# Down projection of a gated block by 26 block products, accumulated in PSUM over all features

## The chip, the cores and the metric

The kernel runs on one core of a Trainium2 chip. The time is the device time of one execution in microseconds, here the median of several executions. Five engines matter. TensorE (PE in the profile) multiplies matrices into PSUM banks. VectorE (DVE), ScalarE (ACT) and GpSimd (POOL) do the elementwise work, and SyncE (SP) issues most of the DMA transfers between HBM and SBUF. Each engine works through its own instructions in order, and semaphores order them against each other.

## The reference

Two branches are computed from one token matrix `x` (2048 tokens, 576 columns), and a gate per token mixes them. The change touches only the second branch, the gated MLP:

```python
def _B_ref(x, w_gate, w_up, w_down):
    g = jnp.einsum("bsd,df->bsf", x, w_gate)
    u = jnp.einsum("bsd,df->bsf", x, w_up)
    h = _gelu(g) * u                              # 2048 x 4608
    return jnp.einsum("bsf,fd->bsd", h, w_down)   # 4608 -> 576

g = _sigmoid((x * gate_w).sum(-1, keepdims=True))
return g * a + (1 - g) * b      # a: linear attention, b: _B_ref
```

All data are float32.

## The kernel before

**Precision.** Every float32 operand of TensorE is split into a high part, rounded to TensorE's format by a ScalarE copy, and a low part, the difference of the value and its high part, by a subtraction on VectorE or GpSimd. A product is then three chains of matmuls: high by high, high by low, low by high.

**Stages.** First come the attention branch's projections, then a mixing stage whose steps are written out by hand in `PLAN`, which also leaves the gated attention result in DRAM (`ga_d`, one tile for each of 16 token tiles of 128). Then comes the gate/up stage: the loop over `CHAINS` (L998), one chain for each token half `p` (two halves, each of two blocks of 512 tokens), feature group `n` (18 groups of 256 features, two blocks of 128) and matrix `m` (`GATE` or `UP`). A chain is one 2x2 block product by seven block products (Strassen-Winograd), seven steps `s1` to `s7` in `gu_steps`. After an `UP` chain the four blocks of h of that half and group are known. The steps form the seven operand sums that the next product needs (L877 to L889) and store them block by block in DRAM (`keep_block`, `h_d`).

**The down stage** (L1053 to L1106) has 84 units: six slices `s` of three feature groups, two token halves `p`, seven products `k`. A unit multiplies a stored sum of h blocks (three groups of 128 features by 512 tokens) by a sum of blocks of `w_down` (three groups by 288 columns): four token tiles of nine matmuls, 36 matmuls of 128x128 by 128x288. For each unit

- `h_load` brings the h sum from DRAM (768 KB) into a raw buffer, through SyncE's queue;
- `h_make` splits it: a ScalarE copy (L966) and a VectorE subtraction (L967), both 1536 wide, into one of five buffers `hb`;
- `d_make` splits the weight sum: a ScalarE copy 864 wide (L946) and two GpSimd subtractions 432 wide (L948), into one of eight buffers `wd`. This is done once per slice and product, and serves both token halves;
- `d_sum` forms the weight sums T1 to T4 on GpSimd (L953), four per slice.

The h operands are made three units ahead of their use. At the end of a unit each of its four token tiles is read out of PSUM. For the first product the sum is copied to a second bank by ScalarE (L1069). For the six others VectorE multiplies the bank by `1 - g`, adds it to an accumulator in SBUF and writes it back (L1073); the accumulators `acc` start as the gated attention result. After the last slice the accumulators go to the output by DMA.

The order of the work is the order in which this program emits it: on each engine `unit(u, 0)`, then `h_make(u + 3)` and the load for u + 6, then `unit(u, 1)`, then the weight work. In the last gate/up chains the tables `D_AT` and `H_AT` place the first units' operand work between the steps.

Of the kernel before, what the change touches and what calls it, by code (L numbers as in the profile page):

```python
# [57 lines left out]
SEQUENCE = (1, 6, 2, 7, 5, 4, 3)  # L58
# [6 lines left out]
def tile_gated_mix(ctx, tc, xt, xs, xn, wk, wv, wq, wo, wgu, wdn, cst, out):  # L65
# [14 lines left out]
    h_d = [[dram.tile([128, 7, 3, BS], F32, name=f"h_d{p}_{i}") for i in range(NF2 // 3)] for p in range(NP)]  # L80
# [488 lines left out]
    nc.vector.tensor_scalar(gate[:, 1], gate[:, 0], -1.0, 1.0, op0=OP.mult, op1=OP.add)  # L569
    query(2, 2)  # L570
# [182 lines left out]
    def g_():  # L753
        nc.scalar.activation(probe, probe, AF.Gelu_apprx_tanh)
# [3 lines left out]
    def open_(k):  # L758
        if k == 0:
            turn.close()  # L760
            weights.close()
            pools["r3"] = mixing.pool("r3p")
            pools["q"] = mixing.pool("qp", bufs=2)
            pools["xc"] = chunks.pool("xcp", bufs=2)
        elif k == 1:
            aheads.close()
            proj.close()
            wgp = mlp.pool("wgp", side="right")
            W.extend(wgp.tile([128, 7, 5, 128], F32R, name=n) for n in ("wg", "wu"))
        else:  # L770
            chunks.close()
            pool = mlp.pool("mid", side="right")
            mid.update((k, pool.tile([128, BS], F32, name=k)) for k in ("p1", "u2", "u3", "e0"))
            es.append(mid["e0"])
            first_steps.extend(gu_steps(*CHAINS[0], first=True))
# [11 lines left out]
    POS = {PRODUCTS[k][0]: i for i, k in enumerate(SEQUENCE)}  # L787
# [3 lines left out]
    last_up = xf[:, 5184:9664].rearrange("p (a b c) -> p a b c", a=7, b=5)  # L791
# [27 lines left out]
    def gu_steps(p, n, m, first=False):  # L819
# [10 lines left out]
        def keep_block(a, src):  # L830
            nc.sync.dma_start(h_d[p][n // 3][:, POS[a], n % 3], src)
# [19 lines left out]
        def s2():  # L851
# [4 lines left out]
            else:  # L856
                up(0, a)
                keep_block(A11, es[0])
# [6 lines left out]
        def s5():  # L865
# [3 lines left out]
            if m == UP:  # L869
                keep_block(A22, es[3])  # L870

        def s4():
# [3 lines left out]
            if m == UP:  # L876
                nc.vector.tensor_tensor(sx[:, 0], es[2], es[3], OP.add)  # L877
                nc.vector.tensor_tensor(sx[:, 1], sx[:, 0], es[0], OP.subtract)
                nc.vector.tensor_tensor(es[2], es[0], es[2], OP.subtract)
                keep_block(S1, sx[:, 0])  # L880
                keep_block(S2, sx[:, 1])
                keep_block(S3, es[2])

        def s3():
# [3 lines left out]
            if m == UP:  # L888
                nc.vector.tensor_tensor(sx[:, 2], es[1], sx[:, 1], OP.subtract)  # L889
                keep_block(A12, es[1])  # L890
                keep_block(S4, sx[:, 2])
# [29 lines left out]
    DG = 6  # L921
    ORDER = (1, 2, 3, 4, 5, 0)
    UNITS = [(s, p, k) for s in range(DG) for p in range(NP) for k in range(7)]
# [8 lines left out]
    wd = [wd_view(xf[:, i * 1728:(i + 1) * 1728]) for i in range(4)]  # L932
    hb = [h_view(v) for v in (xf[:, 9984:13056], xf[:, 13056:16128], wf[1][:, :3072], wf[0][:, :3072], xf[:, 6912:9984])]
    hraw = [f32(xf[:, 16128:17664]).rearrange("p (g c) -> p g c", g=3), e123]
    draw = stage.rearrange("p (i c) -> p i c", i=5)
    D12, D11, D21, D22, DX = range(5)
    DAT = {B11: D11, B21: D21, B22: D22, T1: D11, T2: DX, T3: D12, T4: D21}

    def d_fetch(s):
        nc.sync.dma_start(draw[:, :4], wdn[ORDER[s]].rearrange("p i g c -> p i (g c)"))  # L940

    HALVES = slice(0, 432), slice(432, 864)

    def d_make(s, k):
        w, src = wd[(7 * s + k) % 8], draw[:, DAT[PRODUCTS[SEQUENCE[k]][1]]]
        nc.scalar.activation(w[:, 0], src, AF.Copy)  # L946
        for c in HALVES:
            nc.gpsimd.tensor_tensor(w[:, 1, c], src[:, c], f32(w[:, 0, c]), OP.subtract)  # L948

    def d_sum(t):  # L950
        o, x, y = {T1: (D11, D12, D11), T2: (DX, D22, D11), T3: (D12, D22, D12), T4: (D21, D21, DX)}[t]
        for c in HALVES:
            nc.gpsimd.tensor_tensor(draw[:, o, c], draw[:, x, c], draw[:, y, c], OP.subtract)  # L953

    def raw_of_h(j):
        return hraw[j % 2 if j < 4 else (j - 2) % 3]

    def h_load(j):
        if j < len(UNITS):
            s, p, k = UNITS[j]  # L960
            nc.sync.dma_start(raw_of_h(j), h_d[p][ORDER[s]][:, k])

    def h_make(j):
        if j < len(UNITS):
            h, raw = hb[j % 5], raw_of_h(j)
            nc.scalar.activation(h[:, 0], raw, AF.Copy)  # L966
            nc.vector.tensor_tensor(h[:, 1], raw, f32(h[:, 0]), OP.subtract)  # L967
# [17 lines left out]
    for k in range(2):  # L985
# [3 lines left out]
    D_AT = {(LAST - 2, 0): lambda: d_make(0, 0), (LAST - 2, 4): lambda: d_sum(T1), (LAST - 1, 0): lambda: d_sum(T2),  # L989
            (LAST - 1, 2): lambda: d_make(0, 1), (LAST - 1, 4): lambda: d_make(0, 2), (LAST - 1, 6): lambda: d_sum(T3),  # L990
            (LAST, 4): lambda: d_sum(T4)}
    W_AT, REST = {(0, 4): ((0, 2),), (0, 5): ((4, 6),)}, ((2, 3), (3, 4), (6, 7))
    H_AT = [(LAST - 1, 1), (LAST - 1, 3)]
# [4 lines left out]
    for c, chain in enumerate(CHAINS):  # L998
        for i, step in enumerate(first_steps if c == 0 else gu_steps(*chain)):
# [22 lines left out]
            if (c, i) == (LAST - 4, 0):  # L1022
                d_fetch(0)
            if c == LAST - 2 and i in (0, 4):
                h_load(i // 4)
            if (c, i) in D_AT:
                D_AT[c, i]()
            if (c, i) in H_AT:
                j = H_AT.index((c, i))
                h_make(j)  # L1030
                h_load(2 + j)
# [4 lines left out]
    acc = [dp.tile([128, 4, 4, 288], F32, name=f"acc{p}") for p in range(NP)]  # L1036
    wd += [wd_view(dp.tile([128, 1728], F32R, name=f"wd{i}")) for i in range(4)]
    hraw.append(dp.tile([128, 3, BS], F32, name="hraw"))

    def acc_load(p, t):  # L1040
        i, j = divmod(t, 4)
        nc.sync.dma_start(acc[p][:, 2 * i:2 * i + 2, j], ga_d[p * 8 + t].rearrange("p (n c) -> p n c", n=2))

    h_load(4)
    for t in range(4):
        acc_load(0, t)

    C11, C12, C21, C22 = range(4)
    RESULT = {6: C12, 2: C11, 7: C22, 5: C22, 4: C21, 3: C12}
    FINAL = {2: C11, 5: C22, 4: C21, 3: C12}  # L1050
    sums_of = {}

    def unit(u, q):  # L1053
        s, p, i = UNITS[u]
        k = SEQUENCE[i]
        name = {1: "a", 6: "b", 2: "a", 7: "b", 5: "d", 4: "b", 3: "d"}[k]
        h, w = hb[u % 5], wd[(7 * s + i) % 8]
        c = RESULT.get(k)
        ops = [(hl, wl, g) for hl, wl in ((0, 0), (0, 1), (1, 0)) for g in range(3)]
        for t in (2 * q, 2 * q + 1):  # L1060
            if k in (1, 5):
                sums_of[name, t] = bank()
            y = sums_of[name, t][:, :288]
            for n, (hl, wl, g) in enumerate(ops):
                nc.tensor.matmul(y, h[:, hl, g, t * 128:(t + 1) * 128], w[:, wl, g * 288:(g + 1) * 288],  # L1065
                                 start=k in (1, 5) and n == 0, stop=n == len(ops) - 1, skip_group_check=True)
            if k == 1:
                sums_of["b", t] = bank()
                nc.scalar.activation(sums_of["b", t][:, :288], y, AF.Copy)  # L1069
            else:  # L1070
                st = p * 8 + c // 2 * 4 + t
                o = acc[p][:, c, t]
                nc.vector.scalar_tensor_tensor(o, y, gate[:, 1, st:st + 1], o, op0=OP.mult, op1=OP.add)  # L1073
                if s == DG - 1 and FINAL.get(k) == c:
# [106 lines left out]
```

## Time and profile before

| | |
|---|---|
| runs | 1473.12, 1472.52, 1471.91 us; median 1472.52 |
| profiled execution, span from first to last instruction | 1470.6 us |
| TensorE busy | 1465.0 us |
| VectorE, GpSimd, ScalarE busy | 1038.5, 720.9, 547.2 us |
| HBM read, written | 156.84 MB, 88.28 MB |

The profiled execution is one execution, with a span of 1470.6 us; the time of a run is taken around the whole program and is 1.9 us longer at the median. In the profile's rows PE is a matmul, PEld the loading of its weights, L1065 a line of the kernel, `out<-in` the tiles that an instruction writes and reads; "x84" is a count. A row of windows gives the start and end of the stretch, its length, the busy time of PE, PEld, VectorE, ScalarE and GpSimd with their counts, the granted TensorE clock, the mean busy share of the 16 DMA engines and GB/s. A row by source line gives the shortest, median and longest duration in ns. A row of the timeline gives start, duration, engine, line and operation, and in brackets the idle time before it and what ended that.

### The profile page before, as it was taken

The numbers are of one execution on the slowest core, as the hardware profiler recorded it, in microseconds if no ns is written. First come the engines' busy times: TensorE is split into PE (matmuls) and PEld (weight loads), VectorE is DVE, ScalarE is ACT, GpSimd is POOL, SyncE is SP. The second block draws the span as 40 slices with busy tenths as digits, with TensorE's granted clock in tenths as the row PEclk, the third lists the DMA queues.
The fourth block names the chain that finished last, engine by engine and source line by source line (L and its number), as shares of the span: only waits on it lengthen the run. The fifth ranks groups of instructions, "written<-read, shape, count | busy, mean of one in ns | idle before, by whom it ended". The sixth has DMA issues, their size and how long they took to land.

```text
span 1470.6 us, 21605 instructions
## 1 busy us (share of the span) xinstructions
PE 1465.0 (100%) x8312; PEld 1311.9 (89%) x8312; DVE 1038.5 (71%) x1351; ACT 547.2 (37%) x719; POOL 720.9 (49%) x522
## 2 busy tenths in 40 slices
PE   9999999999999999999999999999999999999999
PEld 9999899888888888888888888888899999999999
DVE  7887898565677655677665677665778777777775
ACT  7555656333322223222223222232254444443431
POOL 1664543456455464465464464462446464463710
PEclk9999999999999999999999999999999999999999
DMA  7564476653333222333222333224796655565563
GB/s 255 160 207 140 161 250 218 238 220 129 108 143 143 108 103 108 112 143 144 94 107 107 123 143 126 103 109 182 263 344 213 218 173 204 169 221 199 175 215 127
DMA packets 100599, 246.56 MB, mean 168 GB/s; under 512 B 9416, under 2 KB 36616, under 8 KB 98320
## 3 DMA queue, kind: packets, MB, share of 16 engines
q1 hardware_dynamic: 97760, 237.91, 46.6%
q10 hardware_dynamic: 2736, 7.28, 1.3%
q8 instruction: 65, 1.06, 0.3%
q14 instruction: 38, 0.31, 0.1%
HBM read 156.84 MB, written 88.28 MB: 167 GB/s over the span
## 4 chain that ended last, share of the span: by engine, by line
PE 98%; DMA 1%; DVE 1%; ACT 0%; SPq 0%; issue 0%; DVEq 0%
PE bank L801 54%; PE bank L1065 27%; PE bank L479 4%; PE pair L728 4%; PE pair L282 2%; PE kpair L282 2%; PE pair L237 2%; PE kpair L237 2%; PE den L667 1%; DMA xn<-xn 0%; DMA raw<-wk 0%; PE pair L634 0%; PE pair L530 0%; DVE e L246 0%; ACT pkh L252 0%
## 5 line engine op out<-in xcount | busy, mean ns | idle before, releaser
L801 PE MATMUL bank<-xo,wg 128*128 128x512 f32 x1764 | 403.7, 389 | 0.0
L801 PEld LDWEIGHTS bank<-xo,wg 128*128 128x128 f32 x1764 | 330.8, 188 | 68.9 <-DVE f L835 0.3
L801 PE MATMUL bank<-xo,wu 128*128 128x512 f32 x1715 | 391.8, 389 | 0.0
L801 PEld LDWEIGHTS bank<-xo,wu 128*128 128x128 f32 x1715 | 321.9, 188 | 66.8
L1073 DVE SCALAR_TENSOR_TENSOR acc<-bank,gate,acc 128x288 f32<-128x288 f32 x288 | 139.9, 512 | 67.1 <-PE bank L1065 64.8
L321 POOL TENSOR_TENSOR stage<-stage 128x384 f32<-128x384 f32 x132 | 153.7, 1185 | 49.0 <-ACT ga L735 23.2
L844 ACT ACTIVATE p<-bank 128x512 f32<-128x512 f32 x72 | 43.0, 597 | 325.2 <-PE bank L801 204.9
L816 POOL TENSOR_TENSOR wg<-stage,wg 128x768 fp32r<-128x768 f32 (+3 forms) x37 | 73.8, 1996 | 164.8 <-ACT wg L815 163.3
L816 POOL TENSOR_TENSOR wu<-stage,wu 128x768 fp32r<-128x768 f32 (+1 forms) x34 | 76.5, 2251 | 141.7 <-ACT wu L815 140.4
L1065 PE MATMUL bank<-wd,xo 128*128 128x288 f32 x1008 | 136.2, 295 | 0.0
L1065 PEld LDWEIGHTS bank<-wd,xo 128*128 128x128 f32 x1008 | 134.4, 188 | 0.0
L948 POOL TENSOR_TENSOR xo<-stage,xo 128x432 fp32r<-128x432 f32 x44 | 65.0, 1498 | 112.7 <-ACT xo L946 84.0
L849 DVE TENSOR_TENSOR u<-bank,p 128x512 f32<-128x512 f32 x72 | 49.4, 686 | 89.0 <-PE bank L801 81.2
L1065 PE MATMUL bank<-xo 128*128 128x288 f32 x792 | 107.0, 295 | 0.2 <-DVE u L838 0.2
L1065 PEld LDWEIGHTS bank<-xo 128*128 128x128 f32 x792 | 105.6, 188 | 0.5 <-DVE u L838 0.4
L948 POOL TENSOR_TENSOR wd<-stage,wd 128x432 fp32r<-128x432 f32 x40 | 59.4, 1510 | 90.1 <-ACT wd L946 72.3
L835 DVE TENSOR_TENSOR f<-bank,u 128x512 f32<-128x512 f32 x54 | 37.2, 691 | 69.2 <-PE bank L801 68.8
L825 ACT ACTIVATE f<-f 128x512 f32<-128x512 f32 x54 | 34.1, 632 | 128.6 <-DVE f L835 128.6
L863 DVE TENSOR_TENSOR u<-bank,u 128x512 f32<-128x512 f32 x72 | 49.8, 692 | 38.1 <-PE bank L801 34.1
L953 POOL TENSOR_TENSOR stage<-stage 128x432 f32<-128x432 f32 x48 | 76.3, 1616 | 0.0
L825 ACT ACTIVATE e<-e 128x512 f32<-128x512 f32 x54 | 34.0, 631 | 91.9 <-DVE e L835 91.9
L835 DVE TENSOR_TENSOR e<-bank,u 128x512 f32<-128x512 f32 x54 | 37.1, 691 | 40.4 <-PE bank L801 39.0
(198 smaller groups left out, 2373.2 us busy)
## 6 DMA issues: line engine op xcount, KB each, us to landing
h_d<-sx SPq DMA_DIRECT2D x108, 256.0 KB, 7.7
stage<-wgu SPq DMA_DIRECT2D x34, 768.0 KB
xo<-h_d SPq DMA_DIRECT2D x29, 768.0 KB, 6.9
e<-h_d SPq DMA_DIRECT2D x28, 768.0 KB, 4.2
hraw<-h_d SPq DMA_DIRECT2D x27, 768.0 KB, 4.1
h_d<-e SPq DMA_DIRECT2D x72, 256.0 KB, 2.0
h_d<-f SPq DMA_DIRECT2D x72, 256.0 KB, 2.0
stage<-wdn SPq DMA_DIRECT2D x6, 1728.0 KB, 9.6
```

Of the source, the lines that this page charges most:

```text
L237: nc.tensor.matmul(out_t[:, :n], xa, kvw[i][:, r, lo:lo + n], start=(k == 0), stop=(k == 13))
L282: nc.tensor.matmul(y[:, n, :KH], a, p[:, n * KH:(n + 1) * KH], start=(k == 0), stop=(k == len(ops) - 1))
L321: nc.gpsimd.tensor_tensor(o, a, b, OP.subtract)
L479: nc.tensor.matmul(ps[:wa.shape[1]], wa, xa, start=(k == 0), stop=(k == len(ops) - 1), skip_group_check=g == 4)
L801: nc.tensor.matmul(ps, w_, x_, start=start and i == 0, stop=i == 6, skip_group_check=not start)
L816: nc.gpsimd.tensor_tensor(w[:, i, 3:5], src[:, :, 0:2], f32(w[:, i, 0:2]), OP.subtract)
L825: nc.scalar.activation(es[i], es[i], AF.Gelu_apprx_tanh)
L835: nc.vector.tensor_tensor(es[i], a, b, OP.add)
L948: nc.gpsimd.tensor_tensor(w[:, 1, c], src[:, c], f32(w[:, 0, c]), OP.subtract)
L953: nc.gpsimd.tensor_tensor(draw[:, o, c], draw[:, x, c], draw[:, y, c], OP.subtract)
L1065: nc.tensor.matmul(y, h[:, hl, g, t * 128:(t + 1) * 128], w[:, wl, g * 288:(g + 1) * 288], start=k in (1, 5) and n == 0, stop=n == len(ops ...
L1073: nc.vector.scalar_tensor_tensor(o, y, gate[:, 1, st:st + 1], o, op0=OP.mult, op1=OP.add)
```

## The change

The down product is taken as one product of a 4x4 by a 4x2 block matrix: four token blocks of 512, four feature blocks of 1152 (nine groups of 128), two column blocks of 288. Instead of six slices by two token halves by seven products there are 26 products, listed in `DOWN`, each over all 1152 features of a block in three units `c`; a unit has the size that it had. That makes 78 units. A line of `DOWN` gives

- the parts of h: one stored sum, or two that are added or subtracted after loading, each with a sign (`-b0`, `+a7+b7`);
- the weight operand, a raw block named by two digits or a sum by a letter;
- whether the product starts a new set of four PSUM banks (`-`), goes on in the banks of the one before (`c`), or goes on from a copy of an earlier product's banks (a number);
- the results (row block, column block) to which VectorE adds the banks when the product is done, with a sign;
- the weight sums formed for it.

So a bank is read out after three units and not after each, and mostly stays open over several products.

In the `UP` steps, `made` replaces the seven stored sums of each half and group by 12 sums for even groups and 13 for odd ones, over all four token blocks; some sums are updated in place in later steps. Since the last two chains belong to group 0 of the second half, two blocks of group 0 are stored beside (`hx_d`) and loaded back with three stored sums before them.

In the down stage `h_sum` joins two loaded parts on VectorE, one unit before `h_make`. `Weights` gives 18 tiles of one weight block each to loads and sums; sums are made on VectorE for products with one part and on GpSimd for those with two. `Weights.make` splits the weight anew for every unit, with one GpSimd subtraction 864 wide. There are four buffers `hb` and four `wd`. Products whose parts are all negative take the sign in the split (a scaled copy and a three-operand VectorE instruction); a read with a sign uses a second column of factors in `probe`.

```diff
+DOWN = """
+-b0 30 - -10 .
+-b2 r c . y=21-31,r=y-30
++b3 21 c +11 .
++a7+b7 y 1 -01 .
++b1 v c +00 v=20+r
++a6-b6 w - +20 w=00+10
++a7+b6 z c . z=w-y
+-a3 10 c +00 .
+-a8+b8 o c -30 o=00+01
++a9+b9 20 c -10 .
+-a2 x 6 +10+30 x=01+w
+-a1 k c -01 k=11+x
++ax+bx 11 c . .
++a7 m c -21 m=x-z
+-a0 01 - -11 .
++a9+b8 q c +10 q=20+o
+-a9+by p c +30 p=q-01
+-b8 n c -31 n=21+q
+-bx s - -21 s=11+31
++by j c . j=p+s
++a4-b4 11 c +31 .
+-a5-b5 u c -01+11 u=30+31
+-a5-b4 t 19 +01-11 t=30+s
++a5 A c -30 A=10+t
+-ay+b6 10 c . .
+-bz l c +20 l=j-t
+"""
...
+        def made(i):
+            e, (s0, s1, s2) = ES[0], (sx[:, k] for k in range(3))
+            if n % 2 == 0 and p == 0:
+                if i == 2:
+                    keep("0", e[2])
+                elif i == 1:
+                    add(s0, e[1], e[3])
+                    keep("1", s0)
+                    sub(s1, e[0], s0)
+                    keep("2", s1)
+                    sub(e[1], e[0], e[1])
+                    keep("3", e[1])
...
+        def sums(self, j):
+            m, c = UNITS[j]
+            for name, x, op, y in DOWN[m].made:
...
+                eng = nc.vector if len(DOWN[m].parts) == 1 else nc.gpsimd
+                eng.tensor_tensor(self.tile(name, c), a, b, OP.add if op == "+" else OP.subtract)
+
+        def make(self, j):
+            m, c = UNITS[j]
+            w, src = wd[j % 4], self.tile(DOWN[m].v, c)
+            nc.scalar.activation(w[:, 0], src, AF.Copy)
+            nc.gpsimd.tensor_tensor(w[:, 1], src, f32(w[:, 0]), OP.subtract)
+            self.drop(j)
...
+    def h_sum(j):
+        if j < len(UNITS) and len(DOWN[UNITS[j][0]].parts) == 2:
...
+            if minus == less:
+                nc.vector.tensor_tensor(a, a, b, OP.add)
+            else:
+                nc.vector.tensor_tensor(a, *((b, a) if minus else (a, b)), OP.subtract)
+            free()
+            h_load()
...
+    def unit(u, half):
+        m, c = UNITS[u]
+        d, first = DOWN[m], not (DOWN[m].goes_on or DOWN[m].seed is not None)
...
+            if c < NK - 1:
+                continue
+            if seeds:
+                nc.scalar.activation(set_of["seed", m][t][:, :288], y, AF.Copy)
+            for minus, i, j in d.reads:
+                st, o = 4 * i + t, acc[:, i, j, t]
+                by = probe[:, 8 + st:9 + st] if minus else gate[:, 1, st:st + 1]
+                nc.vector.scalar_tensor_tensor(o, y, by, o, op0=OP.mult, op1=OP.add)
...
+    for u in range(len(UNITS)):
         unit(u, 0)
+        h_make(u + 3)
+        w_make(u + 3)
+        w_sums(u + 4)
         unit(u, 1)
+        h_sum(u + 4)
+        if u in (1, 3, 6):
+            acc_load((0, 2, 3)[(1, 3, 6).index(u)])
```

Products are numbered from 0 in the order of `DOWN`, units from 0 to 77.

324 lines of the change are left out of this document (201 added, 123 removed).

## The prediction

> **What bounds the kernel now.** I read the page first, for the engine shares and the chain that ended last.
>
> ```profile
> span 1470.6 us, 21605 instructions
> PE 1465.0 (100%) x8312; PEld 1311.9 (89%) x8312; DVE 1038.5 (71%) x1351; ACT 547.2 (37%) x719; POOL 720.9 (49%) x522
> PE bank L801 54%; PE bank L1065 27%; PE bank L479 4%; PE pair L728 4%; PE pair L282 2%; PE kpair L282 2%; PE pair L237 2%; PE kpair L237 2%; PE den L667 1%; DMA xn<-xn 0%; DMA raw<-wk 0%; PE pair L634 0%; PE pair L530 0%; DVE e L246 0%; ACT pkh L252 0%
> ```
>
> TensorE is never idle, and the chain is TensorE throughout. Next the chain in order of time (start, length, instructions), the windows of the gate/up stage, of the down stage and of one piece of it, and the last matmuls of the down stage by source line.
>
> ```profile
> 1068.56 398.82 PE bank L1065 x3006
> 400.00:1000.00 600.00, 600.00 (x2649) 496.82 (x2648) 400.13 (x490) 161.91 (x213) 316.50 (x216) 1.00 0.33 120
> 1065.00:1467.00 402.00, 401.79 (x3028) 401.27 (x3027) 295.36 (x377) 168.93 (x169) 182.25 (x118) 1.00 0.61 206
> 1080.00:1120.00 40.00, 40.00 (x304) 39.87 (x303) 33.62 (x43) 20.97 (x20) 27.62 (x19) 1.00 0.93 332
> L1065 PE MATMUL bank<-xo x792: 288/295/403, 1065.8 to 1433.7; 128*128 128x288 f32 x198
> L1065 PE MATMUL bank<-xo,wg x360: 288/295/302, 1080.5 to 1467.1; 128*128 128x288 f32 x180
> ```
>
> The down stage runs from 1065.8 to 1467.4 us: 401.6 us for 84 units of 36 matmuls, 4.78 us a unit, at the full granted clock (1.00). The other engines must deliver a unit's operands every 4.78 us; now they do (VectorE 295, GpSimd 182, ScalarE 169 us of 402). So fewer units shorten the run only as long as the operands still come at that pace, and the question is what one unit costs VectorE and GpSimd.
>
> **Those two exclude each other.** The same subtraction on VectorE takes 1.75 us or up to 2.6; on GpSimd 1.11 or up to 2.6 (min/median/max).
>
> ```profile
> L967 DVE TENSOR_TENSOR xo<-e,xo x17: 1748/1961/2589, 1055.0 to 1441.6; 128x1536 fp32r<-128x1536 f32 x17
> L953 POOL TENSOR_TENSOR stage<-stage x48: 1107/1124/2656, 1038.2 to 1389.2; 128x432 f32<-128x432 f32 x48
> L1073 DVE SCALAR_TENSOR_TENSOR acc<-bank,gate,acc x288: 499/511/521, 1076.9 to 1467.4; 128x288 f32<-128x288 f32 x144
> ```
>
> The PSUM read L1073 stays at 0.50 to 0.52 us; only VectorE operations with both inputs in SBUF stretch. The timeline shows why.
>
> ```profile
> 1240.96 1.11 POOL L948 TENSOR_TENSOR wd<-stage,wd 128x432 fp32r<-128x432 f32 x1 [4.08 <-ACT wd L946]
> 1241.11 2.59 DVE L967 TENSOR_TENSOR xo<-e,xo 128x1536 fp32r<-128x1536 f32 x1
> 1242.04 2.64 POOL L948 TENSOR_TENSOR wd<-stage,wd 128x432 fp32r<-128x432 f32 x1
> ...
> 721.47 5.31 POOL L321 TENSOR_TENSOR stage<-stage 128x384 f32<-128x384 f32 x4 [0.59 <-DMA stage<-wgu]
> ...
> 721.68 1.39 DVE L877 TENSOR_TENSOR sx<-e 128x512 f32<-128x512 f32 x1
> 723.10 1.38 DVE L878 TENSOR_TENSOR sx<-sx,e 128x512 f32<-128x512 f32 x1
> 724.41 1.50 DVE L879 TENSOR_TENSOR e<-e,e 128x512 f32<-128x512 f32 x1
> ```
>
> The first GpSimd operation ends at 1242.07, VectorE's at 1243.70, 1.63 later; the second GpSimd one at 1244.68, 0.98 after that. Each waits for the whole of the other, and with both queues full (721 us) they take strict turns. So in turns a 1536-wide VectorE operation holds its place 1.63 us, a 432-wide GpSimd one 0.98. Other widths:
>
> ```profile
> L877 DVE TENSOR_TENSOR sx<-f x18: 691/692/694, 333.0 to 1065.9; 128x512 f32<-128x512 f32 x18
> L816 POOL TENSOR_TENSOR wg<-stage,wg x37: 738/1859/2404, 276.2 to 983.3; 128x768 fp32r<-128x768 f32 x16, 128x1024 fp32r<-128x1024 f32 x16, 128x256 fp32r<-128x256 f32 x3, 128x512 fp32r<-128x512 f32 x2
> ```
>
> VectorE: (1.748-0.691)/1024 = 1.03 ns an element, so 864 wide holds 1.63-672*1.03 ns = 0.94 us. GpSimd: (2.404-1.107)/592 = 2.19 ns, so 864 wide holds 0.98+432*2.19 ns = 1.93 us. These are estimates from those rows.
>
> **The change, TensorE.** 26 products of 3 units are 78 units: 78*4.78 = 372.9, less 28.7 us. No other part can shorten a chain that is TensorE throughout.
>
> **What each unit needs.** Counting the scheme's lines: 14 products have one h part, 12 have two, so 114 h loads instead of 84. Singles form their weight sums on VectorE (11, times 3 units = 33), doubles on GpSimd (7, so 21). Before, one split weight served both token halves: 42 weights, 84 half operations, 48 half sums, 132*0.98 = 129 us beside 84*1.63 = 137 of VectorE: 266 of 402. After, every unit splits its own weight: GpSimd 78+21 = 99 operations; VectorE 78 low parts (11 products' by a three-operand operation with a constant, two SBUF inputs, priced alike), 36 h sums, 33 weight sums. Units 0 to 2 and one unit's two weight sums are prepared in the gate/up stage. What is left is 96*1.93 + 111*1.63 + 31*0.94 = 185.3+180.9+29.1 = 395.3 us, one at a time. With TensorE's last unit after it the stage cannot take less than 400.1, against 401.6 now. The 28.7 us are gone before any imperfection.
>
> **The order in which they come.** For a double, VectorE's queue holds: low part of unit u+3, h sum of u+4, low part of u+4. Between the last two ScalarE must copy the sum.
>
> ```profile
> L966 ACT ACTIVATE xo<-e x17: 1472/1480/1493, 1053.5 to 1439.1; 128x1536 fp32r<-128x1536 f32 x17
> L946 ACT ACTIVATE xo<-stage x22: 905/917/932, 1034.6 to 1407.9; 128x864 fp32r<-128x864 f32 x22
> ```
>
> With a hand-over each way of 0.04 (VectorE's L835 in the gate stage ends at 706.31, its gelu starts at 706.35):
>
> ```profile
> 705.62 0.69 DVE L835 TENSOR_TENSOR f<-bank,u 128x512 f32<-128x512 f32 x1 [0.90 <-PE bank L801]
> 706.35 0.63 ACT L825 ACTIVATE f<-f 128x512 f32<-128x512 f32 x1 [4.83 <-DVE f L835]
> ```
>
> - Double with no GpSimd sum (5 products: 3, 9, 12, 20, 24). After the h sum: 1.56 copy; low part 1.63; GpSimd, whose copy (0.92, queued behind) was ready at 2.5, has waited and goes first, 1.93; next h sum 1.63. 6.75 a unit, 20.25 a product.
> - Double with a GpSimd sum (7 products: 5, 6, 8, 15, 16, 21, 22). The sum fills the copy's gap: two turns of 1.63+1.93, 7.12 a unit, 21.4 a product.
> - Single with a VectorE sum: 1.63+0.94+1.93 = 4.50 a unit, so TensorE's 4.78 rules; 14.34 a product. Without one (products 2, 7, 14): 3.56 a unit, 10.7, and 3.6 can be won back.
>
> Can the lookahead hide the doubles? Operands are made three units ahead, 14.3 us. But a product that goes on in the same PSUM banks (`c`) must wait until VectorE has read the one before, and those reads stand behind the low part of u+2 and the h sum of u+3. At 15 boundaries TensorE therefore waits once VectorE is about 3 us late, long before the lookahead is used. That is the new wait; matmuls stand behind it. The reads themselves (24*4 instead of 288) fit into GpSimd's turns, at no cost.
>
> Sum: 14*14.34 + 5*20.25 + 7*21.4 = 200.8+101.3+149.5 = 451.6, less 3*3.6 won back = 440.7 us, +39 us on the stage.
>
> **The rest.** Up steps: 180 sums instead of 144. The 36 more, 0.69 to 1.45 us each, lie beside TensorE (600.00 of 600, VectorE 400.13); I take 0, without cover up to 26*2 = 52 us at 1.45; no gain is possible since TensorE was full. The block stores fall from 252 to 227:
>
> ```profile
> h_d<-sx SPq DMA_DIRECT2D x108, 256.0 KB, 7.7
> ...
> h_d<-e SPq DMA_DIRECT2D x72, 256.0 KB, 2.0
> h_d<-f SPq DMA_DIRECT2D x72, 256.0 KB, 2.0
> ```
>
> Down loads: 114*0.786 + 48*0.442 + 9.4 (accumulator in, result out) = 120 MB; at 332 GB/s for 0.93 share (357 at full) 337 us, under either bound, hidden. ScalarE's bank copies fall from 48 to 12. The end after the last matmul (3.2 us) stays.
>
> **Time.** The profiled execution's span is 1470.6, the median of the runs 1472.5; I keep those 1.9 us. 1472.5+39.1 = 1511.6: I forecast **1511**.
>
> **The rivals.**
> 1. *Gap filled.* GpSimd falls a unit behind and works in ScalarE's copy gap, so doubles without a sum pack to 2*1.63+1.93 = 5.19, 15.6 a product: 5*4.7 = 23 us less, **1488**. For it: in 721 us they pack well. Against: GpSimd's own copy is queued right behind, so it has always caught up. Packed to the floor of 400.1 it is 1471. Chances 0.17 and, for the floor, 0.04.
> 2. *Reads not hidden.* At the ends of doubles the PSUM reads lengthen VectorE's turn: 7*4+2*8 = 44 reads of 0.51, +22 us, **1534**. For it: reads wait for TensorE. Against: GpSimd's 1.93 covers two. Chance 0.13.
> 3. *Not slower: TensorE still rules.* Place: the doubles. It needs a double under 4.78 us a unit, which is so if the two engines' operations overlap; then the stage is 372.9, **1444**. For it: in 1080 to 1120 they were busy 33.6+27.6 us of 40 and TensorE was full. Against: those busy times include the waiting just shown. Chance 0.05.
> 4. *Each turn pays a pause*, 115 ns on 21*4+15*3 = 129 turns of the doubles: +15, **1526**. Against: the blocked GpSimd row ended 0.98 after VectorE, shorter than the 1.11 of a free one. Chance 0.02. The Trainium skill, "SBUF — State Buffer", section "SBUF: two separate sides", has the two share one exclusive lock for a whole instruction and names about 115 ns after VectorE's end, measured there for a DMA's descriptors. On the whole-instruction wait the trace agrees (1.63 and 0.98 us); on the pause it does not.
>
> **How the numbers follow.** The forecast has 0.59. The range 1480 to 1534 leaves out rival 3, the floor, part of rival 1 and the upper half of rival 2, about 0.2. About 0.2% is what a measurement of this kernel can tell from no change (3 us). Faster: rival 3, 0.05; within: the floor, 0.04; the rest slower, 0.91. The forecast's own range is 1500 to 1522.
>
> **What would show it.** In the down window TensorE's busy time is near 373 of 440 with idle before matmuls released by VectorE's reads and low parts; VectorE's 1536-wide median rises from 1.75 to 1.96 in the rows above to over 2.5 us, and GpSimd's 864-wide operations take about 3; both near 85% busy or more. Gate/up stays at 600 of 600. It is wrong if the down stage's TensorE is full, if DMA is the releaser, or if GpSimd's 864-wide means stay near 2.1.

## The result and the profile after

The kernel after takes **1624.37 us** (median of four executions, 1623.26 to 1627.36), the kernel before on the same chip 1472.82 (four, 1471.91 to 1474.49). The ratio is 1.1032, with a 95% interval of 1.1017 to 1.1048: slower, and far above the forecast of 1511 and the range's upper end of 1534. First the page of the kernel after: span, busy times, and the granted clock in 40 slices.

```profile
span 1621.4 us, 21022 instructions
PE 1486.2 (92%) x8096; PEld 1319.2 (81%) x8096; DVE 1192.7 (74%) x1259; ACT 558.3 (34%) x713; POOL 813.9 (50%) x489
PEclk9999999999999999999999999999898989999898
```

TensorE runs 216 matmuls fewer than before and yet is busy 21 us longer, and it is no longer busy throughout. In the last third the clock shows eights. So there are two losses to find: idle time, and matmuls that take longer. The windows of the kernel after (columns as before: length, busy time of TensorE, its loads, VectorE, ScalarE, GpSimd; clock, DMA share, GB/s) are the gate/up piece and the down stage:

```profile
400.00:1000.00 600.00, 565.76 (x2442) 463.56 (x2441) 411.68 (x470) 150.33 (x200) 299.31 (x199) 0.98 0.28 100
1132.00:1618.00 486.00, 407.07 (x2810) 401.96 (x2808) 387.34 (x251) 179.96 (x162) 277.10 (x96) 0.91 0.67 238
```

The gate/up piece, 600.00 of 600 before, has 34 us of idle time. The down stage is 486 long, with 79 idle, and its busy time is 407.1 where 78 units at 4.78 would be 372.9. The down matmuls by source line:

```profile
L1256 PE MATMUL bank<-xo x2124: 288/295/609, 1132.2 to 1617.7; 128*128 128x288 f32 x194
```

The median matmul is the old one (295 ns), the longest twice that (609; 403 before). The waits (engine and line, what it waited for, us in total, times, longest) say what ended the idle time, in the down stage and in the gate/up stage:

```profile
PE bank L1256 <- DVE acc L1266: 73.9, 17, 10.2
...
PE bank L852 <- DVE e L963: 45.1, 16, 3.3
```

In the down stage it is VectorE's PSUM reads, L1266, for 73.9 of the 78.9 us (4.2 more end with ScalarE's copy of a bank set); in the gate/up stage it is a VectorE read of a bank, L963. From the first down matmul, the last one's end, and the sum of the gaps over 0.15 us between matmuls, the whole difference of the spans, 1621.4 - 1470.6 = 150.8 us, divides thus:

| | before | after | difference |
|---|---|---|---|
| up to the first down matmul | 1065.8 | 1132.2 | +66.4: 51.0 idle in 18 gaps of over 2 us, 15.4 longer matmuls |
| down stage | 401.6 | 485.8 | +84.2: -28.7 fewer matmuls, +78.9 idle in 20 gaps, +34.0 longer matmuls |
| after the last matmul | 3.2 | 3.4 | +0.2 |

**The gaps of the gate/up stage.** There is one of 2.5 to 3.3 us per feature group, 16 in all, and two more at the end of the stage. The timeline of the kernel after around one of them (start, length, engine, line, operation; in brackets the idle time before and what ended it):

```profile
526.92 2.09 POOL L867 TENSOR_TENSOR wu<-stage,wu 128x768 fp32r<-128x768 f32 x1 [9.13 <-ACT wu L866]
527.33 2.23 DVE L885 TENSOR_TENSOR sx<-f 128x512 f32<-128x512 f32 x1
...
529.59 1.39 DVE L885 TENSOR_TENSOR sx<-sx,f 128x512 f32<-128x512 f32 x1
530.51 2.73 POOL L867 TENSOR_TENSOR wu<-stage,wu 128x1024 fp32r<-128x1024 f32 x1
530.90 2.88 DVE L885 TENSOR_TENSOR f<-f 128x512 f32<-128x512 f32 x1
...
535.27 1.29 DVE L963 TENSOR_TENSOR e<-bank,mid 128x512 f32<-128x512 f32 x2
536.01 5.29 PE L852 MATMUL bank<-xo,wg 128*128 128x512 f32 x22 [2.93 <-DVE e L963]
```

Three of the new sums at the end of an `UP` chain (L885, 0.69 us when alone) meet GpSimd's split of the next `UP` weights (L867 and L868) and take 2.23, 1.39 and 2.88. Behind them in VectorE's queue stand the first reads of the next chain's banks, the last of them L963, and a later product of that chain wants such a bank: TensorE waits 2.93.

**The cycle of the doubles.** The timeline of the kernel after, first in products with a GpSimd sum, then in one without:

```profile
1225.44 3.60 DVE L1150 TENSOR_TENSOR hraw<-hraw,xo 128x1536 f32<-128x1536 f32 x1
...
1239.57 3.58 DVE L1148 TENSOR_TENSOR mid<-mid,wg 128x1536 f32<-128x1536 f32 x1
1241.49 3.52 POOL L1103 TENSOR_TENSOR vt<-vt,vt 128x864 f32<-128x864 f32 x1
1243.26 1.48 ACT L1162 ACTIVATE xo<-mid 128x1536 fp32r<-128x1536 f32 x1 [4.27 <-DVE mid L1148]
...
1244.78 1.86 DVE L1163 TENSOR_TENSOR xo<-mid,xo 128x1536 fp32r<-128x1536 f32 x1 [1.63 <-ACT xo L1162]
...
1246.05 2.44 POOL L1109 TENSOR_TENSOR xo<-vt,xo 128x864 fp32r<-128x864 f32 x1 [1.03 <-ACT xo L1108]
1246.56 3.55 DVE L1148 TENSOR_TENSOR hraw<-hraw,xo 128x1536 f32<-128x1536 f32 x1
...
1250.03 0.93 DVE L1266 SCALAR_TENSOR_TENSOR acc<-bank,gate,acc 128x288 f32<-128x288 f32 x2
...
1250.69 7.04 PE L1256 MATMUL bank<-xo,wu 128*128 128x288 f32 x36 [10.20 <-DVE acc L1266]
...
1271.89 4.94 PE L1256 MATMUL bank<-xo,wu 128*128 128x288 f32 x36
...
1350.52 3.61 DVE L1148 TENSOR_TENSOR mid<-mid,wg 128x1536 f32<-128x1536 f32 x1
...
1355.77 1.76 DVE L1163 TENSOR_TENSOR xo<-mid,xo 128x1536 fp32r<-128x1536 f32 x1 [1.64 <-ACT xo L1162]
1356.63 2.76 POOL L1109 TENSOR_TENSOR xo<-vt,xo 128x864 fp32r<-128x864 f32 x1 [4.11 <-ACT xo L1108]
1357.44 3.56 DVE L1148 TENSOR_TENSOR hraw<-hraw,xo 128x1536 f32<-128x1536 f32 x1
```

From h sum to h sum it is 6.99 us (1239.57 to 1246.56), over three units 7.04 each (1225.44 to 1246.56), and without a GpSimd sum 6.92 (1350.52 to 1357.44), against TensorE's 4.78. At 1250.69 the product goes on in banks that VectorE has just read (L1266): 10.20 us of idle time have gathered by then. The 36 matmuls after it take 7.04 us, those at 1271.89, with no gap before them, 4.94. Two groups of the kernel after in the down stage (count | busy us, mean ns of one | idle before):

```profile
L1109 POOL TENSOR_TENSOR xo<-vt,xo 128x864 fp32r<-128x864 f32 x52 | 140.5, 2703 | 135.8 <-ACT xo L1108 128.6 <-DMA wg<-h_d 4.1 <-DMA vt<-wdn 2.0
...
L1266 DVE SCALAR_TENSOR_TENSOR acc<-bank,gate,acc 128x288 f32<-128x288 f32 x48 | 22.8, 505 | 16.0 <-PE bank L1256 16.0
```

Of the 36 h sums 25 take 3.55 to 3.62 us, which is the 1.63 + 1.93 of the prediction; the other 11 take 1.74 to 2.76. A low part of h in a double (L1163) starts behind ScalarE's copy and is hardly stretched (1.76 and 1.86 above). The PSUM reads keep their 0.505.

### The profile page after: what moved, and what is told of

Its sections match the earlier page's. It is cut to its first block, busy times and chain, and to the rows that moved or that the text cites. A ratio compares the mean times of both kernels' runs of the same rounds, so it can differ in the third digit from the quotient of the medians.

```text
span 1621.4 us, 21022 instructions
## 1 busy us (share of the span) xinstructions
PE 1486.2 (92%) x8096; PEld 1319.2 (81%) x8096; DVE 1192.7 (74%) x1259; ACT 558.3 (34%) x713; POOL 813.9 (50%) x489
## 5 line engine op out<-in xcount | busy, mean ns | idle before, releaser
L852 PE MATMUL bank<-xo,wg 128*128 128x512 f32 x1764 | 418.7, 397 | 45.1 <-DVE e L963 45.1
L1256 PE MATMUL bank<-xo 128*128 128x288 f32 x2124 | 316.7, 313 | 68.7 <-DVE acc L1266 63.7
L852 PEld LDWEIGHTS bank<-xo,wu 128*128 128x128 f32 x1715 | 322.0, 188 | 66.9
L1256 PEld LDWEIGHTS bank<-xo 128*128 128x128 f32 x2124 | 310.3, 205 | 73.4 <-issue 57.1
L1109 POOL TENSOR_TENSOR xo<-vt,xo 128x864 fp32r<-128x864 f32 x52 | 140.5, 2703 | 135.8 <-ACT xo L1108 128.6
L972 ACT ACTIVATE mid<-bank 128x512 f32<-128x512 f32 x72 | 43.1, 598 | 328.3 <-PE bank L852 224.1
L867 POOL TENSOR_TENSOR wg<-stage,wg 128x768 fp32r<-128x768 f32 (+3 forms) x37 | 73.4, 1983 | 163.1 <-ACT wg L866 161.7
L867 POOL TENSOR_TENSOR wu<-stage,wu 128x768 fp32r<-128x768 f32 (+1 forms) x34 | 79.4, 2335 | 141.5 <-ACT wu L866 140.2
L1109 POOL TENSOR_TENSOR xo<-stage,xo 128x864 fp32r<-128x864 f32 x26 | 69.0, 2656 | 117.2 <-ACT xo L1108 88.7
L977 DVE TENSOR_TENSOR mid<-bank,mid 128x512 f32<-128x512 f32 x72 | 49.3, 685 | 93.2 <-PE bank L852 84.5
L1256 PE MATMUL bank<-xo,wu 128*128 128x288 f32 x684 | 95.7, 299 | 10.2 <-DVE acc L1266 10.2
L1256 PEld LDWEIGHTS bank<-xo,wu 128*128 128x128 f32 x684 | 93.6, 192 | 10.4 <-issue 10.4
L963 DVE TENSOR_TENSOR f<-bank,mid 128x512 f32<-128x512 f32 x54 | 37.3, 691 | 70.4 <-PE bank L852 70.0
L966 DVE TENSOR_TENSOR mid<-bank,mid 128x512 f32<-128x512 f32 x108 | 74.0, 685 | 18.9 <-PE bank L852 17.0
L876 ACT ACTIVATE e<-e 128x512 f32<-128x512 f32 x54 | 33.8, 628 | 150.8 <-DVE e L963 150.8
L991 DVE TENSOR_TENSOR mid<-bank,mid 128x512 f32<-128x512 f32 x72 | 49.8, 692 | 38.5 <-PE bank L852 34.4
L879 DVE TENSOR_TENSOR e<-mid,e 128x512 f32<-128x512 f32 x54 | 64.8, 1199 | 1.9
L963 DVE TENSOR_TENSOR e<-bank,mid 128x512 f32<-128x512 f32 x54 | 35.7, 687 | 36.1 <-PE bank L852 28.9
```

The costliest lines, as they stand in the source:

```text
L852: nc.tensor.matmul(ps, w_, x_, start=start and i == 0, stop=i == 6, skip_group_check=not start)
L867: nc.gpsimd.tensor_tensor(w[:, i, 3:5], src[:, :, 0:2], f32(w[:, i, 0:2]), OP.subtract)
L876: nc.scalar.activation(es[i], es[i], AF.Gelu_apprx_tanh)
L879: nc.vector.tensor_tensor(es[i], v, es[i], OP.mult)
L963: nc.vector.tensor_tensor(es[i], a, b, OP.add)
L966: nc.vector.tensor_tensor(tmp, a, b, OP.add)
```

## The experiments

The theory after the result: the gate/up loss comes from sums that meet the weight split, the down loss from VectorE and GpSimd taking turns. Against it stood: the 36 more sums as such are too much for the gate/up stage; the down loss is VectorE's chain with ScalarE, or the place of the reads, and not the turns. Each time is one execution unless a median is named. In the table, down stage and idle time are taken as above; "longer" is what the stage has beyond idle time and 372.9 us.

| kernel | time | first down matmul | down stage | idle | longer |
|---|---|---|---|---|---|
| after | 1624.4 (median) | 1132.2 | 485.8 | 78.9 | 34.0 |
| e1_split_late | 1564.4 | 1075.2 | 484.0 | 79.1 | 32.0 |
| e2_low_once | 1555.3 | 1137.2 | 412.3 | 30.0 | 9.4 |
| e3_halves | 1600.2 | 1136.3 | 458.3 | 63.2 | 22.1 |
| e4_sums_vector | 1648.7 | 1137.7 | 505.8 | 97.2 | 35.7 |
| e5_reads_first | 1609.0 | 1137.4 | 466.4 | 68.5 | 25.0 |
| e10_sum_two_ahead | 1588.4 | 1136.1 | 446.6 | 56.3 | 17.4 |
| e6_all_vector | 1604.8 | 1137.3 | 461.7 | 63.8 | 25.0 |
| e8_all | 1496.1 | 1077.1 | 412.9 | 28.6 | 11.4 |
| e9_all_rf | 1500.8 | 1076.0 | 418.9 | 32.1 | 13.9 |
| e12_all_two_rf | 1490.7 | 1077.4 | 407.6 | 25.2 | 9.5 |
| e13_all_two | 1490.9 | 1076.4 | 408.9 | 25.7 | 10.3 |
| e14_all_two_rf_timed | 1489.65 (median) | 1075.0 | 408.6 | 27.2 | 8.5 |

The gate/up code is the same in after, e2 to e6 and e10, and its end lies between 1132.2 and 1137.7: differences between single executions below some 5 us are read as nothing.

**The weight split later (e1).** The split of the next `UP` weights comes after the fourth step of the chain instead of the first; the 180 sums stay.

```diff
-            if i == 0 and c in at:
+            if c in at and i == (3 if c > 5 and at[c][1] == UP else 0):
```

> The split of the next up weights (GpSimd, four operations, about 7 us) is issued three steps later in each gate chain, so that it no longer meets VectorE's sums at the end of the up chain before. Theory A (the sums are drawn out by turns with GpSimd and so the gate chain's fourth bank is read late): the 16 gaps of 2.5 to 3.3 us in the gate/up stage (45 us together) go, and with them the slow matmuls behind some of them (about 12 us); the down stage stays at 486 us; about 1567 us in all. Rival (there are simply more sums in VectorE's queue): the gaps shrink by less than a third, over 1605 us.

The gate/up stage ends 57.0 us earlier, and its idle time is 6.5 instead of 51.0. The window and the timeline of this kernel at the same place in the stage:

```profile
400.00:1000.00 600.00, 600.00 (x2649) 496.82 (x2648) 395.56 (x512) 159.49 (x214) 313.58 (x218) 1.00 0.30 109
```

```profile
517.37 0.69 DVE L885 TENSOR_TENSOR sx<-f 128x512 f32<-128x512 f32 x1
...
518.70 0.68 DVE L885 TENSOR_TENSOR f<-f 128x512 f32<-128x512 f32 x1
...
523.37 1.86 POOL L867 TENSOR_TENSOR wu<-stage,wu 128x768 fp32r<-128x768 f32 x1 [15.55 <-ACT wu L866]
```

The sums are done at 519.4, before the split begins, at 0.69 us each, and TensorE is full again. So it was the meeting, not the number of sums. The stage still ends 9.4 us later than before; that rest was not followed.

**GpSimd's low parts only once (e2).** GpSimd's subtraction of the weight split runs for units 0 to 3 alone.

```diff
-            nc.gpsimd.tensor_tensor(w[:, 1], src, f32(w[:, 0]), OP.subtract)
+            if j < 4:
+                nc.gpsimd.tensor_tensor(w[:, 1], src, f32(w[:, 0]), OP.subtract)
```

> Left out: GpSimd makes the low part of the weight only for units 0 to 3, later units use those old low parts. Theory A (VectorE and GpSimd take turns, and that sets the down stage): the down stage falls from 486 us to about 395 (singles at TensorE's pace, doubles without a sum 4.8, with a sum 5.2 us a unit), its idle time from 79 to under 20 us, and the matmuls run at the full clock; about 1530 us in all. Rival (the place of the PSUM reads behind other VectorE work in the queue is enough): idle time stays over 50 us, the time over 1590.

The down stage falls by 73.5 us, to 412.3: the largest effect of any single edit on it, and less than expected. The window and the timeline of this kernel (whose lines are numbered one higher from the edit on) show what is left:

```profile
1137.00:1550.00 413.00, 382.46 (x2810) 379.05 (x2808) 291.09 (x251) 177.05 (x162) 64.10 (x22) 0.97 0.77 281
```

```profile
1227.35 1.75 DVE L1149 TENSOR_TENSOR e<-e,wg 128x1536 f32<-128x1536 f32 x1
...
1230.74 1.76 DVE L1164 TENSOR_TENSOR wu<-e,wu 128x1536 fp32r<-128x1536 f32 x1 [1.64 <-ACT wu L1163]
1232.42 1.75 DVE L1149 TENSOR_TENSOR mid<-mid,wg 128x1536 f32<-128x1536 f32 x1
```

GpSimd keeps its weight sums (most of the 64.10 us), but no operation of it runs beside these rows. Without one a double still takes 5.07 us a unit, over 4.78: h sum, 1.64 of waiting for ScalarE's copy, low part. The turns are the larger cause, the copy's gap a second one.

**Smaller turns (e3).** The same subtraction in two halves of 432.

```diff
-            nc.gpsimd.tensor_tensor(w[:, 1], src, f32(w[:, 0]), OP.subtract)
+            for c in (slice(0, 432), slice(432, 864)):
+                nc.gpsimd.tensor_tensor(w[:, 1, c], src[:, c], f32(w[:, 0, c]), OP.subtract)
```

> GpSimd's low part of the weight in two operations 432 wide instead of one 864 wide: each holds VectorE up 0.98 instead of 1.93 us, the sum of the two is the same. Theory A (total of the turns): doubles without a GpSimd sum 5.8 instead of 6.75 us a unit, so 14 us less, the rest unchanged: about 1608 us. Rival (the length of one hold delays the reads): every boundary gains about 1 us and the clock recovers, 35 us less or more: under 1590.

The down stage falls by 27.5 us. The time lies between the two expectations, so this run does not tell them apart; it shows that the length of one GpSimd operation matters, at the same work.

**All weight sums on VectorE (e4).**

```diff
-                eng = nc.vector if len(DOWN[m].parts) == 1 else nc.gpsimd
+                eng = nc.vector
```

> The weight sums of the seven products with two parts move from GpSimd (1.93 us) to VectorE (0.94 us). Theory A (total of the turns): 21 units by 0.99 us less, with the clock behind it 21 to 30 us: about 1598 us. Rival (VectorE's own chain with ScalarE's copy in it is the limit, and GpSimd's sum only filled the gap): a unit takes 1.56+1.63+1.93+1.63+0.94 = 7.7 instead of 7.1 us, 12 us more: about 1636.

This became slower by 20 us in the down stage; the gain that the theory of the turns expected did not come, and the rival of the chain with ScalarE was right in direction; the whole run lost 24 us, twice its 12. The timeline of this kernel:

```profile
1244.95 1.74 DVE L1148 TENSOR_TENSOR e<-e,wg 128x1536 f32<-128x1536 f32 x1
...
1248.33 1.76 DVE L1163 TENSOR_TENSOR wu<-e,wu 128x1536 fp32r<-128x1536 f32 x1 [1.63 <-ACT wu L1162]
...
1250.01 2.86 DVE L1103 TENSOR_TENSOR vt<-vt,vt 128x864 f32<-128x864 f32 x1
1252.79 1.74 DVE L1148 TENSOR_TENSOR mid<-mid,wg 128x1536 f32<-128x1536 f32 x1
```

A unit takes 7.84 us here (1244.95 to 1252.79). On GpSimd the sum had lain in the 1.63 us gap of the copy; now the gap is empty, and the sum, which waits out GpSimd's split (2.86), is added to the line.

**The four reads first (e5).** In a product's last unit both halves of `unit` come before `h_make`, and the h sum for u + 3 moves behind these reads; each h sum still comes ahead of its own low part.

```diff
         unit(u, 0)
+        if u % 3 == 2:
+            unit(u, 1)
+            h_sum(u + 3)
         h_make(u + 3)
         w_make(u + 3)
         w_sums(u + 4)
-        unit(u, 1)
-        h_sum(u + 4)
+        if u % 3 != 2:
+            unit(u, 1)
+        if u % 3 != 1:
+            h_sum(u + 4)
```

> In the last unit of each product VectorE reads all four banks before it goes on with later units' low part, weight sum and h sum; nothing else changes. Theory A (VectorE's turns with GpSimd and ScalarE's copy between its h sum and its low part set the pace, the reads are only where TensorE feels it): the lag turns into a wait for operands instead, the down stage gains what the three units of lookahead can take up, 10 to 25 us of 486, about 1605 us. Rival (the reads' place in the queue is the cause): most of the 79 us idle and the clock lost with it go, the down stage under 420 us, under 1560 in all.

The down stage falls by 19.4 us. This is the 10 to 25 us of the theory: the place of the reads counts, as the new wait of the prediction says, but most of the idle time stays (68.5 of 78.9 us).

**The h sum two units ahead (e10).** ScalarE's copy is then ready before VectorE comes to the low part.

```diff
-        h_sum(u + 4)
+        h_sum(u + 5)
```

> The h sum is taken one unit earlier (for u+5 instead of u+4), so that the low part that follows it in VectorE's queue belongs to the unit before and does not wait for ScalarE's copy of that sum. Theory A: doubles without a GpSimd sum go from 6.75 to 5.2 us a unit (15 units, 23 us) and the clock with it, those with one stay at 7.1 since GpSimd's sum filled the gap; 25 to 35 us less, about 1592 us. Rival (GpSimd gets its turn anyway, the two together are the limit): under 10 us.

The down stage falls by 39.2 us and the whole run by 35.9, where 25 to 35 were expected. The weight sums of GpSimd in this kernel's timeline, one per unit, show that the doubles with a GpSimd sum do not get shorter:

```profile
1224.69 3.58 POOL L1103 TENSOR_TENSOR vt<-vt,vt 128x864 f32<-128x864 f32 x1
...
1231.77 3.57 POOL L1103 TENSOR_TENSOR stage<-stage 128x864 f32<-128x864 f32 x1
...
1238.83 3.52 POOL L1103 TENSOR_TENSOR vt<-vt,vt 128x864 f32<-128x864 f32 x1
```

They come 7.08 and 7.06 us apart. With no wait for a copy in the line, these units still cost two turns of 1.63 + 1.93 = 7.12.

**All weight work on VectorE, same order (e6).** The edits are e4's and this one:

```diff
-            nc.gpsimd.tensor_tensor(w[:, 1], src, f32(w[:, 0]), OP.subtract)
+            nc.vector.tensor_tensor(w[:, 1], src, f32(w[:, 0]), OP.subtract)
```

> GpSimd does nothing in the down stage: the weights' low parts and all weight sums are VectorE's, in the same order. Theory A: a 864 wide operation costs the pair 0.94 instead of 1.93 us; doubles 6.0 us a unit without and 7.0 with a sum (copy gap 1.64 included), singles 3.6: about 430 us for the down stage with the clock, 1565 in all. Rival (VectorE is the engine that is short, and the work moved to it makes it worse): the down stage over 486 us, over 1625 in all.

The direction was right and the size was not: 24.1 us off the down stage, where some 55 were expected. The window of this kernel:

```profile
1137.00:1599.00 462.00, 398.07 (x2811) 392.87 (x2809) 363.71 (x347) 177.35 (x162) 0.00 (x0) 0.93 0.70 251
```

With GpSimd empty VectorE has 364 us of work in 462 and is idle for 98. The largest of its waits in that window is the one for ScalarE's copy of the h sum:

```profile
DVE xo L1163 <- ACT xo L1162: 40.0, 25, 5.0
```

**e6 with the order mended and e1's edit (e8, e9, e12, e13, e14).** e8 forms the h sum right after `h_make`; e9 is e8 with the reads ahead of that; e13 has e10's edit in place of e8's; e12 is e13 with the reads first; e14 repeats e12 with more executions. The order of e12:

```diff
         unit(u, 0)
+        if u % 3 == 2:
+            unit(u, 1)
         h_make(u + 3)
         w_make(u + 3)
         w_sums(u + 4)
-        unit(u, 1)
-        h_sum(u + 4)
+        if u % 3 != 2:
+            unit(u, 1)
+        h_sum(u + 5)
```

> As e6, and the h sum for u+4 directly behind the low part of u+3, with the weight's low part and sums after it, so that ScalarE's copy runs beside them; and the split of the up weights three steps later as in e1. Theory A: doubles 5.0 us a unit without and 5.9 with a sum, singles at TensorE's 4.78; the down stage about 395 us, the gate/up stage 60 us shorter; about 1470 us in all. Rival (what is lost comes from the reads' place): the down stage stays over 430 us, over 1505 in all.

> As e8, and in the last unit of each product the four PSUM reads come before VectorE's later work. With the turns gone, theory A: VectorE alone (about 360 us of work against TensorE's 373) leaves boundary waits of 1 to 5 us, 29 us together in e8; reads first let the lookahead take up part of them, 10 to 20 us less, about 1480 us. Rival (VectorE now waits for TensorE's fourth bank in every product and loses more than it gains): over 1496.

> As e9, with the h sum a whole unit earlier (u+5, at the end of unit u) instead of directly behind the low part. Theory A: ScalarE's copy (1.64 us with its hand-overs) then never stands between two VectorE operations; in e8 it is covered by 0.94 or 1.9 us of weight work, so 0.7 us a unit is left for 15 units, 10 us less than e9, about 1472. Rival: that cover was enough, the same as e9 within 3 us.

> As e12 with the reads where they were. Theory A: 10 us less than e8, about 1486 us; rival: the same as e8 within 3 us.

> The fastest of the variants (all weight work on VectorE, h sum two units ahead, reads first, up split three steps later) timed against the kernel before. Theory A: what is left is VectorE's own 360 us of work with waits at a few boundaries, 25 us idle and 10 us of slow clock beside TensorE's 373, and 10 us at the end of the gate/up stage: 1490 us, 1.2% over before. Rival (the one look was a lucky one or a disturbed one): outside 1485 to 1496.

From e6 to e13 the down stage falls by 52.8 us, which is the price of the copy's place in that order (e1's edit, which e13 has too, moved the down stage by 1.8 us alone). e8 and e12 stayed 26 and 19 us above what was expected. e9 was expected to gain 10 to 20 us on e8 and lost 4.7, as its rival had it; e13 gained 5.2 on e8, between the 10 of its theory and the 3 of its rival. With the reads first e9 has a down stage 6.0 us longer than e8, and e12 one 1.3 us shorter than e13: once the turns are gone the place of the reads brings no gain that these runs can tell. The best, e14, takes 1489.65 us (1489.03 to 1490.15) against 1472.27, a ratio of 1.012 (1.0103 to 1.0136). Its window:

```profile
1076.00:1485.00 409.00, 380.37 (x2802) 378.26 (x2800) 359.95 (x345) 179.76 (x162) 0.00 (x0) 0.97 0.77 282
```

VectorE alone now has 360 us beside TensorE's 373. The stage is 7 us longer than the 401.6 of before, and the gate/up stage ends 9 us later. Of its 27.2 us of idle time 26.6 still end with VectorE's reads (L1266), 6.9 of them before the second product; what held VectorE up each time was not separated. No version that was run beats the kernel before.

## Why the prediction was wrong

The direction was right and the size was not. Two steps failed: the sums of the `UP` steps, put at 0, and the down stage outside the doubles, put at TensorE's pace and full clock. Counted on TensorE, the sum of 1511.6 lacks three terms: 66.4 in the gate/up stage, 34.0 for longer matmuls in the down stage, and 78.9 - (440.7 - 372.9) = 11.1 of idle time there. 1511.6 + 66.4 + 34.0 + 11.1 = 1623.1; the profiled execution took 1623.3.

1. **TensorE, -28.7: right.** The median matmul is unchanged.
2. **VectorE and GpSimd exclude each other: right, with its sizes.** The h sum beside a GpSimd operation takes 3.6 us where 1.63 + 1.93 = 3.56 were worked out; in e4, where GpSimd has nothing to do at that point, 1.74.
3. **The order of the doubles: right.** 7.12 a unit with a GpSimd sum, measured 6.99 (7.08 and 7.06 in e10); 6.75 without, measured 6.92. That the copy's gap and the turns are two causes is shown by e2, which removes most of the turns and keeps the gap, and e10, which removes the gap and keeps the turns.
4. **The new wait: right.** TensorE's idle time ends with L1266 in 17 waits of 73.9 us together; e5, which moves those reads, wins 19.4. Left out was the first boundary: 9.64 us before the second product, as VectorE still had sums of the last `UP` chain and then waited 3.84 us for weights. Without it the idle time is 69.3, against 67.8 predicted; that these agree so well is in part luck (see 5).
5. **The down stage outside the doubles, at TensorE's pace and full clock: wrong, by 45.1.** The prediction worked out 68 us of idle time in some 15 places, and kept 4.78 us for each unit behind them. The matmuls took 34.0 longer; the 7.04 us above are one such unit. But 34.0 is not the price of the clock: 26.1 of it lie in the twelve doubles, where VectorE's cycle sets the pace and a faster matmul would in part have waited instead. No run separates this. Counted on VectorE, from the start of one low part of h to the next, the 36 steps to units of doubles take 254.5 us, near the 250.8 predicted. The other 38 take 202.5, where the prediction's prices (4.78 a unit with a weight sum, 3.58 without) make 170.8: 31.7 more. And the first of all these low parts, for unit 3, starts 11.0 us after the first down matmul. With 3.7 more in the doubles and 1.2 less at the end, that is the miss of some 45. Part of the 31.7 is explained in 7; the rest was not followed.
6. **The up-step sums at 0: wrong, by 66.4, the largest miss.** The prediction's cover for them was VectorE's 400 of 600 us. But the sums stand in a row, ahead of a read that frees a bank, just where GpSimd splits weights; the row of 721 us that the prediction itself quotes shows what then happens to such sums. A share of a stage was taken for the state of one place. e1 shows the cause for 57.0 of the 66.4. The price "without cover" that the prediction did name, up to 52, is near the 51.0 of idle time, but came from another reckoning (its "26*2" stands for 36 sums at 1.45 us, 52.2).
7. **DMA hidden: right. PSUM reads hidden: right in the doubles, wrong in the singles.** The DMA share is 0.67, and no wait for DMA stands among TensorE's. In the doubles the reads of a product's end fall between the h sums at 1225.44 and 1246.56, and three units still take no more than three times 7.12. In singles with a weight sum (timeline of the kernel after) they lengthen the cycle:

```profile
1473.80 1.74 DVE L1163 TENSOR_TENSOR xo<-wg,xo 128x1536 fp32r<-128x1536 f32 x1
...
1478.30 1.75 DVE L1163 TENSOR_TENSOR wu<-wg,wu 128x1536 fp32r<-128x1536 f32 x1
...
1482.81 0.93 DVE L1266 SCALAR_TENSOR_TENSOR acc<-bank,probe,acc 128x288 f32<-128x288 f32 x2
1483.66 1.74 DVE L1163 TENSOR_TENSOR xo<-xo 128x1536 fp32r<-128x1536 f32 x1
```

From 1473.80 to 1478.30 it is the predicted 4.50; to 1483.66, with two reads in it, 5.36. With four reads a product takes VectorE 3*4.50 + 2*0.86 = 15.22 us, more than TensorE's 14.34, so in such a product VectorE sets the pace where the prediction let TensorE rule.

Of the rivals none came: the gap was not filled in doubles without a sum (6.92, not 5.19); the reads cost nothing at the ends of the doubles, where that rival had placed them; TensorE did not rule; and a pause of 115 ns per turn would make 7.12 into 7.35, where 6.99 to 7.08 were measured. Of the signs, the releaser and GpSimd's 864-wide duration (2.70 for about 3) came as told. "VectorE's 1536-wide over 2.5 us" holds for the h sums alone, not for the low parts. "Both near 85% busy" does not hold: VectorE is busy 387 of 486 us (80%), GpSimd 277 (57%); both wait for ScalarE's copies. "Gate/up stays at 600 of 600" failed. The range was too narrow for one reason: both ends kept the gate/up stage, the clock and TensorE's pace in the singles as they were, although the prediction had a bound of 52 for the first.

## What to carry to other kernels

Work put "beside a full engine" is priced at its place: look in the timeline for what runs on the engine that it excludes, and for what stands behind it in its own queue; a busy share of 67% says nothing about that. Where TensorE sets the pace, a gap that a change opens can be charged twice, once as idle time and again in the matmuls behind it: e1 took 44.5 us of idle time out of the gate/up stage and won 57.0. A sum of idle time is a lower bound there. And when the number of operands per matmul grows, look first for the engine that makes them: after the turns, the copy's wait and the meeting had all been removed, VectorE's 360 us still stood beside TensorE's 373.

## What the runs showed of the hardware

**TensorE's clock falls after a gap.** In the kernel before, with no gap over 0.21 us in the down stage, no 288-column matmul took over 403 ns. In the kernel after each of the down stage's twelve gaps of 3.6 us or more is followed by 11 to 24 matmuls of over 440 and up to 609 ns, twice the median. The gap need not be that long. TensorE's timeline in e8, where the gap at 1147.94 is the first for 50 us:

```profile
1138.53 7.32 PE L1256 MATMUL bank<-xo 128*128 128x288 f32 x54
1147.94 8.87 PE L1256 MATMUL bank<-xo 128*128 128x288 f32 x54 [2.09 <-DVE acc L1266]
...
1415.69 9.53 PE L1256 MATMUL bank<-xo 128*128 128x288 f32 x70 [3.43 <-DVE acc L1266]
```

The same 54 matmuls take 1.55 us more after a gap of 2.09 us; after one of 3.43 the 70 matmuls run at 0.136 us each, as the first 54 do. So it is not the length of the gap alone that decides. The trace also holds the granted clock. Up to the last matmul of e8 and of the kernel after its low stretches last 3.41 us, or two or three times that, and all lie on one grid of such windows. Four windows of e8 on that grid (columns as in the windows above):

```profile
1144.37:1147.78 3.41, 1.49 (x12) 1.25 (x10) 3.41 (x4) 1.69 (x2) 0.00 (x0) 1.00 1.02 413
1147.78:1151.19 3.41, 3.25 (x13) 3.25 (x14) 3.41 (x4) 0.72 (x1) 0.00 (x0) 0.50 0.99 361
1410.60:1414.02 3.42, 1.66 (x13) 1.43 (x11) 3.42 (x3) 0.63 (x1) 0.00 (x0) 1.00 1.00 310
1414.02:1417.43 3.41, 1.74 (x13) 1.74 (x14) 3.41 (x5) 1.78 (x2) 0.00 (x0) 1.00 0.97 355
```

The gap of 2.09 us lies almost whole in one window: TensorE is busy 1.49 of 3.41 us (44%), and the next window has half the clock. The gap of 3.43 us is shared by two, busy 1.66 and 1.74 us (49% and 51%), and the clock stays full. In the kernel after, every full-clock window with TensorE busy up to 42.5% is followed by a half-clock one, and none busy 44.4% or more is. Over all traces of this case a window busy under 43% was always followed by half the clock, and one over 49% never.

The Trainium skill, "TensorE: Matmul & The Clock Gate", section "Part 1: The HAM clock gate (the "warmup" mystery)", has a gate that halves the clock after an idle window of about 3.4 us and opens it after a busy one, the windows running freely, so that the phase matters. The traces agree on the half rate (0.50 granted, 609 for 295 ns) and on the windows of 3.41 us; but a window need not be idle throughout, as the one busy for 44% shows. So the short rule of the Trainium skill, in "HAM oscillation — how this bites in real kernels", that no gap should exceed some 3.4 us, is not safe here.

**The turns cost no pause.** In the rows of the kernel after from 1239.57 on, the four operations of a unit and the next h sum end at 1243.15, 1245.01, 1246.64, 1248.49 and 1250.11: 1.86 for GpSimd's sum, 1.63 for the low part, 1.85 for GpSimd's split, 1.62 for the h sum. An operation that was held back until the other engine ended thus takes no longer than the estimates of the prediction (1.93 and 1.63), and for VectorE less than the 1.75 of an operation that nothing holds back (in e2); the five ends are the whole cycle.
